# Attention and a squared-ReLU network in one program: integer weight splitting without the GpSimd sum, early queries turned by TensorE, copies whose engine the list picks

## The chip, the cores and the metric

The kernel runs on one core of a Trainium2 chip. Its engines work beside each other: TensorE (PE for matrix products, PEld for its weight loads), VectorE (DVE), ScalarE (ACT), GpSimd (POOL), and SyncE (SP), from whose queue all transfers start. The metric is the device time of one execution in microseconds (us).

## The reference

For 8 batches of 8 heads, 576 tokens and head dimension 64, the kernel computes a feature-map attention and passes the result, as 4608 tokens of width 512, through two matrix products with a squared ReLU between them.

```python
def phi(x):
    proj = np.einsum('bhsd,df->bhsf', x, w_phi)               # w_phi: 64 x 128
    proj = proj - np.max(np.abs(proj), axis=-1, keepdims=True)
    return np.concatenate([np.exp(proj), np.exp(-proj)], axis=-1)
q_p, k_p = (phi(q), phi(k))
kv = np.einsum('bhsf,bhsd->bhfd', k_p, v)
z = np.sum(k_p, axis=2)
num = np.einsum('bhsf,bhfd->bhsd', q_p, kv)
den = np.einsum('bhsf,bhf->bhs', q_p, z)[..., None] + 1e-06
attn = num / den                                              # then tokens x 512
h = x @ w_in                                                  # w_in: 512 x 2048
out = np.maximum(h, 0.0) ** 2 @ w_out                         # w_out: 2048 x 512
```

The weights w_in and w_out reach the kernel as 64-bit floating point, seen as pairs of 32-bit words.

## The kernel before

**Tiling.** Heads go in 32 pairs of two. A batch is four pairs. The network works on 18 chunks of 256 tokens, and on 8 slices of 256 features in each: 144 units, each a first product (gemm1, line 960, 24 products of half precision) and a second (gemm2, line 991, 12 products). A unit of chunk 0 needs slice f of both weights ready, and the attention of batch 0.

**Weights.** `prep` (line 400) makes one slice of w_in or w_out, 16 in all, from a raw tile of 1 MB: ACT takes the size of the upper word (`size`, line 421) and the low word as a number (`low`, 432), DVE shifts (`shift`, 424) and adds the sign (`join`, 428), POOL adds the rounded low part (`round_`, 435). After that, a slice of w_in has its largest value taken (453), goes through `power` (a PE product and four small DVE steps) and is split in two halves (ACT 457, DVE 459); a slice of w_out is split in two or three parts (ACT 477, POOL at the helper line 288, DVE 484).

**Attention.** The first six pairs go through `early` (line 605), the others through `visit` and `late`, which stand between the units of the network. In `early` the keys are projected (538, 544), shifted by their largest absolute value and put through the exponential (`keys`), multiplied with the values (594, 599) and with ones (626), and the sums turned (`flip`, 638). The queries are projected with tokens on the partitions (`q_main` 653, `q_tail` 659), so that DVE can take the largest value of each token (664, 668). Then `q_proj` projects them once more, with features on the partitions (682), and subtracts the largest values by products with a negative identity (`nident`, 691), in two halves of 288 tokens; ACT puts each half through two exponentials (698, 700) and the numerators (708) and denominators (726) follow. `tokens` (758) divides and writes the half-precision ring that gemm1 reads; for the first five pairs its product runs on POOL.

**What sets the order.** Every step is an `Op` of a `Plan` with an engine, a duration in us, its predecessors, its buffers and a rank. `Plan.order` is a list scheduler: each engine takes, of the steps that are ready, the one with the lowest rank; PE adds `STAY` to steps of another tiling mode, and a lock stretches DVE and POOL steps that meet. `improve` repeats it with shifted ranks and keeps the shortest plan. The order of the instructions on every engine is fixed by this plan before the program runs. Attention pairs are ranked 4.5 us apart, weight slices from 16.0 in steps of 1.0, units of the network from 36.0 in steps of 1.0.

Of the kernel before, what the change touches and what calls it, by code (L numbers as in the profile page):

```python
# [39 lines left out]
SH = S // 2  # L40
# [8 lines left out]
STAY = 6.0  # L49
TRIALS, SEED, MOVED = 400, 1, 70.0  # L50
WITH_DVE = 16
# [12 lines left out]
class Op:  # L64
    __slots__ = ("n", "eng", "us", "fn", "after", "uses", "rank", "land", "mode", "lock", "start", "end", "left", "next")

    def __init__(self, n, eng, us, fn, after, uses, rank, land, mode, lock):
        self.n, self.eng, self.us, self.fn, self.rank, self.land = n, eng, us, fn, rank, land
        self.mode, self.lock = mode, lock
        self.after, self.uses = [a for a in after if a is not None], list(uses)  # L70
        self.start = self.end = None


class Plan:

# [14 lines left out]
    def add(self, eng, us, fn, after=(), uses=(), rank=0.0, land=0.0, mode=WHOLE, lock=None):  # L90
        op = Op(len(self.ops), eng, us, fn, after, uses, rank, land, mode if isinstance(mode, tuple) else (mode, mode), lock)
        self.ops.append(op)
        return op
# [39 lines left out]
    def improve(self, trials, seed):  # L133
# [4 lines left out]
        for n in range(trials):  # L138
# [6 lines left out]
            if best is None or length <= best:  # L145
                best, plan = length, order
            else:
                for op, rank in old:
                    op.rank = rank
        return plan  # L150

    def order(self):
# [19 lines left out]
        def release(op, least=0.0):  # L172
            at = least
            for a in op.after:
                hop = self.HOP[a.eng] if a.eng != op.eng or a.land else 0.0
                at = max(at, a.end + a.land + hop)
            for tag, n in alone(op):
                at = max(at, open_at.get(tag, 0.0))
            heapq.heappush(waiting[op.eng], (at, op.rank, op.n))
# [5 lines left out]
        while done < len(self.ops):  # L185
            best = None
            for e in self.HOP:
                if not waiting[e] and not ready[e]:
                    continue
                t = free[e] if ready[e] else max(free[e], waiting[e][0][0])  # L190
                if best is None or t < best[0]:
                    best = t, e
            t, e = best
            while waiting[e] and waiting[e][0][0] <= t:
                _, rank, n = heapq.heappop(waiting[e])
                heapq.heappush(ready[e], (rank, n))
# [10 lines left out]
            op.start, op.end = t, t + op.us * (COLD if e == "PE" and t < 125.0 else 1.0)  # L207
            if op.lock is not None:
                if e == "POOL":
                    op.end = max(op.end, locked["DVE"] + op.us)  # L210
                else:
                    op.end += min(op.lock, max(0.0, locked["POOL"] - t))
# [44 lines left out]

def dve_us(n):
# [16 lines left out]
def tile_kernel(ctx, tc, qp, kp, vp, w_phi, w_in, w_out, out):  # L275
# [13 lines left out]

    def tiles(pool, tag, shape, dtype, bufs, first=0):  # L290
# [4 lines left out]
    nident = cp.tile([128, 128], F32, name="nident")  # L295
# [21 lines left out]
    pt_ = tiles(at, "pt", [128, 2, S], F32, 1, EARLY)  # L317
# [38 lines left out]
    for h in range(2):  # L356
# [5 lines left out]
    minus = P.add("DVE", 0.25, lambda: V.tensor_scalar(out=nident, in0=ident, scalar1=-1.0, scalar2=None, op0=ALU.mult),  # L362
                  [pool_start], [], 0.8)
# [5 lines left out]
    def power(src, dst, top, after, uses, rank):  # L369
# [15 lines left out]
        a = P.add("PE", 0.22, gather, after, key + [("pn", ("pw", n))], rank)  # L385
# [14 lines left out]
    def prep(n, f, of_in, rank):  # L400
# [22 lines left out]
        def shift():  # L423
            V.tensor_scalar(out=u(), in0=u(), scalar1=3, scalar2=0x7FFFFFF8,
                            op0=ALU.logical_shift_left, op1=ALU.bitwise_and)

        def join():
            V.scalar_tensor_tensor(out=u(), in0=high_w(), scalar=word(0x80000000), in1=u(),
                                   op0=ALU.bitwise_and, op1=ALU.bitwise_or)

        def low():
            A.activation(out=low_w(), in_=low_w().bitcast(U32), func=AF.Copy, scale=2.0 ** -29)

        def round_():
            G.tensor_tensor(out=u(), in0=u(), in1=low_w(), op=ALU.add)
# [10 lines left out]
        pool_prep.append(o)  # L446
        if of_in:
# [7 lines left out]
            o = home_read[home] = P.add("ACT", 1.25, most, [o], key, rank)  # L455
# [6 lines left out]
        else:  # L462
# [20 lines left out]
            if f < NFP - 2:  # L483
                last.append(P.add("DVE", 0.75, lambda: V.tensor_copy(out=wout[f][2], in_=value(2)), [o], key, rank, lock=0.45))  # L484
# [12 lines left out]
    def batch_scale(b, rank):  # L497
        last = []
        for i in range(NP):
            p = b * NP + i  # L500
            last.append(P.add("ACT", act_us(640) + 0.1, lambda p=p, i=i: A.activation(
# [20 lines left out]
        scale_of[b] = P.add("DVE", 0.5, tokens, [o], [], rank)  # L522
# [82 lines left out]
    def early(p):  # L605


        base, free = PER_PAIR * p, p < BANKS
# [24 lines left out]
        o = P.add("ACT", act_us(384), lambda: A.activation(out=kvs_[p], in_=pv_["s", p][:, 0:384], func=AF.Copy),  # L633
                  [o], [("pv", ("s", p)), ("kvs", p)], R(2.6))

        def flip():
# [4 lines left out]
        kz = P.add("ACT", act_us(384), lambda: A.activation(  # L641
            out=kz_[p], in_=pv_["t", p][:, 0:384], func=AF.Copy), [o], [("pv", ("t", p)), ("kz", p)], R(3.1))
# [3 lines left out]
        most = []  # L646
        q_to = lambda h: flat(ph_[2 * p + h]) if free else pp_["qt", p][:, h, :]
        q_use = [("ph", 2 * p + h) if free else ("pp", ("qt", p)) for h in range(2)]

# [11 lines left out]

        o = P.add("PE", 1.0, q_main, [q_load[p]], [("q", p)] + q_use, R(1.0), mode=ROWS)
        for h in range(2):
            most.append(P.add("DVE", dve_us(512), lambda h=h: V.tensor_reduce(
                out=qm_[p][:, 4 * h:4 * h + 4], in_=q_to(h).rearrange("p (t f) -> p t f", t=4),
                op=ALU.max, axis=AX.X, apply_absolute_value=True), [o], [q_use[h], ("qm", p)], R(1.1)))
        o = P.add("PE", 0.27, q_tail, [q_load[p]], [("q", p), ("pn", ("qt", p))], R(1.0), mode=COLS)
        most.append(P.add("DVE", dve_us(128), lambda: V.tensor_reduce(
            out=qm_[p][:, 8:9], in_=pn_["qt", p][:, 0:128], op=ALU.max, axis=AX.X,
            apply_absolute_value=True), [o], [("pn", ("qt", p)), ("qm", p)], R(1.1)))  # L670
# [4 lines left out]
        for c in range(2):  # L675
            n = 2 * p + c
            cs = slice(SH * c, SH * c + SH)
            pq = ("pp", ("q", n))

            def q_proj(n=n, cs=cs):  # L680
# [3 lines left out]
                for h in range(2):  # L684
                    for t in range(5):
                        lo, hi = max(cs.start, 128 * t), min(cs.stop, 128 * t + 128)
                        if lo < hi:

                            i, r, d = (4 * h + t, 0, lo - 128 * t) if t < 4 else (8, 64 * h, 64 * h)
                            rows = slice(r, 128 if t < 4 else r + 64)  # L690
                            PE.matmul(out=pp_["q", n][:, h, lo - cs.start:hi - cs.start],  # L691
# [391 lines left out]
```

## Time and profile before

| | |
|---|---|
| time, median of 3 runs | 1085.27 us (1084.39 to 1086.54) |
| the profiled execution: its own time | 1087.95 us |
| its span, from the first to the last instruction | 1085.8 us |
| PE busy | 1053.6 us (97%) |
| DVE busy | 744.8 us (69%) |
| ACT busy | 634.8 us (58%) |
| POOL busy | 183.4 us (17%) |
| mean granted clock of TensorE | 0.987 of full speed |

An engine's busy time is the time in which one of its instructions ran. The profile names the wait before an instruction and the engine whose work ended it. The granted clock is the share of full speed (2.4 GHz) that TensorE was given in a stretch; 0.5 is 1.2 GHz.

### The profile page before, as it was taken

What the parts mean: (1) busy time and instruction counts of PE and PEld (TensorE: products, weight loads), DVE (VectorE), ACT (ScalarE), POOL (GpSimd) and SP (SyncE); (2) the same over time, 40 slices, a digit from 0 to 9 for tenths busy, and PEclk for the clock granted to TensorE, in tenths of its full rate; (3) what the DMA queues carried; (4) which work ended last, traced back from release to release, by engine and by line L of the source; (5) the groups of instructions that cost most, each with busy time, mean ns of one, the idle gap of its engine ahead of it and who ended that gap; (6) DMA issues with size and microseconds to landing.
All of it is one profiled execution on the core that took longest, in us unless ns stands there. A gap on an engine that the chain in (4) does not pass through costs nothing.

```text
span 1085.8 us, 19895 instructions
## 1 busy us (share of the span) xinstructions
PE 1053.6 (97%) x7788; PEld 723.2 (67%) x7882; DVE 744.8 (69%) x1543; ACT 634.8 (58%) x1125; POOL 183.4 (17%) x87
## 2 busy tenths in 40 slices
PE   7997999999999999999999999999999999999997
PEld 5664666666666666666666666666666666777774
DVE  6588998888887887868777787867786865111111
ACT  6897864556566665666566666665555655333232
POOL 2344442111011111101111111111101111000000
PEclk9897999999999999999999999999999999999999
DMA  9643330222212222222112122222110101000000
GB/s 326 238 137 104 124 122 32 55 75 56 75 55 75 56 56 75 56 64 67 59 41 58 50 74 56 75 56 75 44 55 27 51 17 30 11 21 20 1 20 20
DMA packets 68289, 73.50 MB, mean 68 GB/s; under 512 B 36836, under 2 KB 41828, under 8 KB 68196
## 3 DMA queue, kind: packets, MB, share of 16 engines
q1 hardware_dynamic: 68196, 72.23, 21.8%
q8 instruction: 62, 1.02, 0.4%
q14 instruction: 31, 0.25, 0.1%
HBM read 59.18 MB, written 12.99 MB: 66 GB/s over the span
## 4 chain that ended last, share of the span: by engine, by line
PE 89%; DVE 4%; DMA 2%; ACT 2%; issue 2%; SPq 0%; POOL 0%; DVEq 0%; ACTq 0%; POOLq 0%
PE po L991 35%; PE ph L960 34%; PE pv L594 5%; PE pn L812 3%; PE pp L881 3%; PE pp L538 3%; PE pv L812 2%; PE pp L691 1%; PE pv L599 1%; DMA v<-in_vp_dram 1%; PE pn L544 1%; DMA raw0i<-in_w_in_dram 1%; DVE win L459 1%; DVE wl L484 1%; PE pn L708 1%
## 5 line engine op out<-in xcount | busy, mean ns | idle before, releaser
L960 PE MATMUL ph<-ring,win 128*128 128x256 f16 x3456 | 400.6, 273 | 2.6 <-DVE win L459 2.6
L960 PEld LDWEIGHTS <-win 128*128 128x128 f16 x3456 | 337.3, 98 | 69.8 <-issue 3.3
L969 ACT ACTIVATE r<-ph,cw 128x512 f32<-128x512 f32 x144 | 98.9, 687 | 239.0 <-PE ph L960 238.7
L894 POOL PARTITION_ALL_REDUCE mx<-pt x52 | 114.2, 2197 | 626.6 <-ACT pt L888 525.9
L288 DVE TENSOR_TENSOR gl<-ph,gh 128x512 bf16<-128x512 f32 x144 | 98.7, 686 | 157.8 <-ACT ph L978 154.8
L991 PE MATMUL po<-wh,gh 128*128 128x512 f32 x432 | 128.6, 419 | 0.0
L991 PE MATMUL po<-wl,gl 128*128 128x512 bf16 x420 | 110.2, 379 | 0.7
L991 PE MATMUL po<-wl,gh 128*128 128x512 bf16 x373 | 100.2, 381 | 3.8
L991 PEld LDWEIGHTS <-gl 128*128 128x128 bf16 x576 | 56.0, 97 | 69.6
L991 PEld LDWEIGHTS <-gh 128*128 128x128 bf16 x576 | 44.8, 98 | 74.1 <-issue 39.5
L971 ACT ACTIVATE gh<-r 128x512 fp32r<-128x512 f32 x144 | 90.8, 630 | 4.6
L991 PEld LDWEIGHTS po<-wh,gh 128*128 128x128 f32 x432 | 74.0, 189 | 18.6 <-issue 4.9
L991 PE MATMUL po<-wout,gh 128*128 128x512 f32 (+1 forms) x273 | 74.8, 405 | 1.2
L978 ACT ACTIVATE ph<-r 128x512 f32<-128x512 f32 x128 | 74.6, 583 | 0.0
L594 PE MATMUL pv<-e,v 128*64 128x256 f32 x512 | 64.3, 395 | 0.0
L834 ACT ACTIVATE n<-pn 128x320 f32<-128x320 f32 x26 | 11.4, 437 | 90.1 <-PE pn L812 90.1
L908 DVE SCALAR_TENSOR_TENSOR pt<-qe,zc,pt 128x576 f32<-128x576 f32 x52 | 42.3, 813 | 22.2 <-ACT pt L906 21.8
L560 ACT ACTIVATE e<-e 128x512 f32<-128x512 f32 x64 | 39.8, 621 | 24.8 <-DVE e L557 24.8
L288 DVE TENSOR_TENSOR qe<-pt,mx 128x576 f32<-128x576 f32 x52 | 39.2, 754 | 19.7 <-POOL mx L894 19.4
L594 PEld LDWEIGHTS pv<-e,v 128*64 128x64 f32 x512 | 37.0, 143 | 16.9 <-issue 3.8
L845 DVE STREAM_TRANSPOSE kvs<-pv 128x256 f32<-128x256 f32 x26 | 11.6, 445 | 45.8 <-PE pv L812 45.0
L906 ACT ACTIVATE pt<-qe,zc 128x576 f32<-128x576 f32 x52 | 40.0, 773 | 4.2
(204 smaller groups left out, 1483.4 us busy)
## 6 DMA issues: line engine op xcount, KB each, us to landing
v<-in_vp_dram SPq DMA_DIRECT2D x32, 320.0 KB
k<-in_kp_dram SPq DMA_DIRECT2D x32, 288.0 KB
q<-in_qp_dram SPq DMA_DIRECT2D x32, 288.0 KB
rb<-rd SPq DMA_DIRECT2D x64, 144.0 KB
out_dram<-o SPq DMA_DIRECT2D x36, 256.0 KB
td<-kvs SPq DMA_DIRECT2D x26, 128.0 KB
kz<-td SPq DMA_DIRECT2D x208, 16.0 KB
raw0i<-in_w_in_dram SPq DMA_DIRECT2D x1, 1024.0 KB
```

The lines of the kernel that those rows point to most:

```text
L288: eng.tensor_tensor(out=out_, in0=a, in1=b_, op=ALU.subtract)
L560: o = P.add("ACT", act_us(512), lambda n=n: A.activation(out=e_[n][:, :, 1, :], in_=e_[n][:, :, 0, :], func=AF.Exp, scale=-1.0), [o], [("e ...
L594: PE.matmul(out=to[64 * h:64 * h + 64, 0:256], lhsT=v_[p][:, t, h, :], rhs=e_[2 * p + h][:, t].rearrange("p s f -> p (s f)"), start=t == 0 ...
L812: PE.matmul(out=to[64 * h:64 * h + 64, :], lhsT=kz_[n][:, 128 * s_ + 64 * h:128 * s_ + 64 * h + 64], rhs=qe_[2 * n + h].rearrange("p (s x) ...
L894: o = P.add("POOL", par_us(S), lambda n=n, h=h: G.partition_all_reduce(mx_[n], pt_[p][:, h, :], channels=128, reduce_op=bass_isa.ReduceOp. ...
L906: o = P.add("ACT", act_us(S, 1), lambda h=h, qe=qe, y=y: A.activation(out=y(), in_=qe(0), func=AF.Copy, scale=zc_[p][:, 2 * h:2 * h + 1]), ...
L908: o = P.add("DVE", dve_us(S), lambda h=h, qe=qe, y=y: V.scalar_tensor_tensor(out=y(), in0=qe(1), scalar=zc_[p][:, 2 * h + 1:2 * h + 2], in ...
L960: PE.matmul(out=ph[:, j, :], lhsT=win[w][:, t, 128 * ff:128 * ff + 128], rhs=ring[half][x][:, t, c0:c0 + T], start=k == 0, stop=k == 3 * K ...
L969: o = P.add("ACT", act_us(512, 1), lambda: A.activation(out=r_[n], in_=ph_[bank], func=AF.Relu, scale=cw[:, f, 0:1]), [g1], [("ph", bank), ...
L971: sq = P.add("ACT", act_us(512), lambda: A.activation(out=gh_[n], in_=r_[n], func=AF.Square), [o], [("r", n), ("gh", n)], Q)
L978: o = P.add("ACT", act_us(512), lambda: A.activation(out=ph_[bank], in_=r_[n], func=AF.Square), [sq], [("ph", bank), ("r", n)], Q)
L991: PE.matmul(out=po_[po[i][1]], lhsT=g[:, j, 128 * i:128 * i + 128], rhs=w[:, j, :], start=(ff == 0 and s == 0), stop=(ff == 2 * NFP - 1 an ...
```

## The change

Three things change in what the program computes with, and one in how the plan is made.

**Weight words.** The steps `shift` and `round_` go. `low` makes a number from 0 to 7 of the low word in one ACT step (a scale and an offset, rounded to an integer), a new DVE step `ends` joins it with the sign of the upper word, in place of the raw low words, and `join` shifts the size by three bits and joins both, in one DVE step.

**Early queries.** `q_proj` goes, and `nident` with it. DVE subtracts the largest value from the projection that has tokens on the partitions (`less`, into `pt`), and TensorE turns the result by 12 transposes a pair (`q_turn`). ACT reads the turned halves of 288 from the same PSUM tile.

**Engines of copies.** `Plan.add` takes a second way for a step (`other`), on another engine. The list offers the step to both; the second engine sees it `LATER` = 2.0 us later, and whichever takes it first keeps it. It stands for the copies out of PSUM (ACT or DVE), the third part of w_out, the first half of the ring, the second squaring in the network (ACT first, DVE second; before, DVE for the first 16 units) and `tokens` of the first five pairs (DVE first, POOL second). Some durations in the plan are new too.

```diff
-        def shift():
-            V.tensor_scalar(out=u(), in0=u(), scalar1=3, scalar2=0x7FFFFFF8,
-                            op0=ALU.logical_shift_left, op1=ALU.bitwise_and)
+        def low():
+            A.activation(out=low_w(), in_=low_w().bitcast(U32), func=AF.Copy, scale=0.875 * 2.0 ** -29, bias=0.4995)
+
+        def ends():
+            V.scalar_tensor_tensor(out=low_w(), in0=high_w(), scalar=word(0x80000000), in1=low_w(),
+                                   op0=ALU.bitwise_and, op1=ALU.bitwise_or)
         def join():
-            V.scalar_tensor_tensor(out=u(), in0=high_w(), scalar=word(0x80000000), in1=u(),
-                                   op0=ALU.bitwise_and, op1=ALU.bitwise_or)
-        def low():
-            A.activation(out=low_w(), in_=low_w().bitcast(U32), func=AF.Copy, scale=2.0 ** -29)
-        def round_():
-            G.tensor_tensor(out=u(), in0=u(), in1=low_w(), op=ALU.add)
+            V.scalar_tensor_tensor(out=u(), in0=u(), scalar=3, in1=low_w(),
+                                   op0=ALU.logical_shift_left, op1=ALU.bitwise_or)
...
         l = P.add("ACT", 1.14, low, [ld], [], rank)
+        l = P.add("DVE", 1.22, ends, [l], [], rank, lock=4.0)
         o = P.add("ACT", 1.14, size, [ld], key, rank)
-        o = P.add("DVE", 0.70, shift, [o], key, rank, lock=0.45)
-        o = P.add("DVE", 1.22, join, [o], key, rank, lock=4.0)
-        o = P.add("POOL", 2.42, round_, [o, l], key, rank, lock=0.0)
+        o = P.add("DVE", 1.22, join, [o, l], key, rank, lock=4.0)
...
+        def most_of(src, i, n, o, use):
+            x = lambda: src().rearrange("p (t f) -> p t f", t=n)
+            o = P.add("DVE", dve_us(128 * n), lambda: V.tensor_reduce(
+                out=qm_[p][:, i:i + n], in_=x(), op=ALU.max, axis=AX.X, apply_absolute_value=True), [o], use + [("qm", p)], R(1.1))
+            less.append(P.add("DVE", dve_us(128 * n), lambda: V.tensor_tensor(
+                out=flat(pt_[p])[:, 128 * i:128 * (i + n)].rearrange("p (t f) -> p t f", t=n), in0=x(),
+                in1=qm_[p][:, i:i + n].unsqueeze(2).to_broadcast([128, n, 128]), op=ALU.subtract),
+                [o], use + [("qm", p), ("pt", p)], R(1.1)))
...
-                    PE.matmul(out=pp_["q", n][:, h, 0:SH], lhsT=wst[64 * h:64 * h + 64, :],
-                              rhs=q_[p][64 * h:64 * h + 64, cs], start=True, stop=False)
...
-                            PE.matmul(out=pp_["q", n][:, h, lo - cs.start:hi - cs.start],
-                                      lhsT=qm_[p][rows, i:i + 1].to_broadcast([rows.stop - r, 128]),
-                                      rhs=nident[rows, d:d + hi - lo], start=False, stop=hi == cs.stop)
+                    for t in range(3 - c):
+                        PE.transpose(pp_["q", n][:, h, 128 * t:128 * t + 128], ut(4 * h + 2 * c + t), ident)
+                if c:
+                    for h in range(2):
+                        rows = slice(64 * h, 64 * h + 64)
+                        PE.transpose(pp_["q", n][:, h, 256:320], ut(8)[rows, :], ident[rows, rows])
...
+    def copy(n, to, of):
+        return (("ACT", out_us(n), lambda: A.activation(out=to(), in_=of(), func=AF.Copy)),
+                ("DVE", dve_us(n), lambda: V.tensor_copy(out=to(), in_=of()), None))
```

The first place in the order is TensorE on the queries of pair 0 (`pp` is the PSUM tile of the half, `qm` the largest values, `pt` the new tile of differences). Before, the first half:

```order
L682 MATMUL pp_264<-q_118,wraw 128x288 x2
L691 MATMUL pp_264<-nident,qm_171 128x128 x2
L691 MATMUL pp_264<-nident,qm_171 128x32
L691 MATMUL pp_264<-nident,qm_171 128x128 x2
L691 MATMUL pp_264<-nident,qm_171 128x32
L638 MATMUL pv_284<-ident,kvs_275 128x128 x3
```

And now both halves, in the order of the program:

```order
L714 MATMUL pp_221<-ident,pt_187 128x128 x6
L624 MATMUL pv_199<-et_182,v_119 64x256 x2
...
L714 MATMUL pp_307<-ident,pt_187 128x128 x4
L718 MATMUL pp_307<-ident,pt_187 128x64 x2
L664 MATMUL pv_317<-ident,kvs_281 128x128 x3
```

Eight products of a half, of which the profile shows 16 records, became six transposes.

The second place is TensorE just ahead of the first unit of the network (`win` is w_in's first half, `ring` the tokens; 538 and 563 are pair 5's keys, 708 and 733 numerators, 726 and 750 denominators, 594 and 626 values and ones). Before:

```order
L708 MATMUL pn_1065<-qe_981,kz_983 64x288 x4
L594 MATMUL pv_1076<-e_1029,v_342 64x256
...
L653 MATMUL pp_1090<-wraw,q_882 128x128 x8
...
L599 MATMUL pv_1076<-et_930,v_342 64x256 x2
...
L626 MATMUL pv_1076<-et_930,mask 32x128 x4
L659 MATMUL pn_1150<-wraw,q_882 64x128 x2
L960 LDWEIGHTS win_77
```

Now:

```order
L714 MATMUL pp_995<-ident,pt_880 128x128 x4
L718 MATMUL pp_995<-ident,pt_880 128x64 x2
L733 MATMUL pn_1017<-qe_974,kz_976 64x288 x4
L563 MATMUL pp_1026<-wraw,k_690 128x128 x8
L733 MATMUL pv_1039<-qe_1010,kz_976 64x288 x4
L750 MATMUL pn_1050<-qe_974,kz_976 32x288
...
L986 LDWEIGHTS win_76
```

The values, the ones and the query projection of pair 5 stood before the first unit and now stand behind it.

The third place is DVE around a slice of the weights (`raw3i` is slice 3 of w_in, `raw1o` slice 1 of w_out, `u` the joined words). Before:

```order
L459 SCALAR_TENSOR_TENSOR win_78<-u_458,cw,win_77 128x4x256
L668 TENSOR_REDUCE qm_868<-pn_877 128x1
L424 TENSOR_SCALAR u_880<-u_880 128x1024
L428 SCALAR_TENSOR_TENSOR u_880<-raw2o,u_880 128x1024
L564 TENSOR_REDUCE kmt_928<-pn_901 128x1
```

Now:

```order
L456 SCALAR_TENSOR_TENSOR raw3i<-raw3i 128x1024
L691 TENSOR_REDUCE qm_631<-pn_760 128x1
L483 SCALAR_TENSOR_TENSOR win_77<-u_360,cw,win_76 128x4x256
L693 TENSOR_TENSOR pt_688<-pn_760,qm_631 128x128
L582 TENSOR_TENSOR e_797<-po_622,km_739 128x4x128
L456 SCALAR_TENSOR_TENSOR raw1o<-raw1o 128x1024
L460 SCALAR_TENSOR_TENSOR u_787<-u_787,raw1o 128x1024
L589 TENSOR_REDUCE kmt_835<-pn_822 128x1
L460 SCALAR_TENSOR_TENSOR u_808<-u_808,raw3i 128x1024
```

A slice has two joins on DVE (456, 460) in place of a shift and a join, the differences of the queries (693) stand among them, and POOL has no step between the joins and ACT.

## Rows read from the trace of the kernel before

**Rows 1.** Busy time by stage: stretch, length, PE, PEld, DVE, ACT, POOL, clock, DMA.

```profile
0.00:22.00 22.00, 15.28 (x157) 12.05 (x159) 12.24 (x24) 12.78 (x22) 2.99 (x7) 0.92 0.92 332
22.00:109.60 87.60, 78.62 (x785) 52.52 (x783) 66.67 (x105) 72.55 (x123) 36.43 (x18) 0.88 0.50 166
109.60:165.40 55.80, 51.62 (x383) 35.31 (x386) 51.88 (x79) 41.99 (x65) 27.36 (x11) 1.00 0.37 119
...
200.00:1000.00 800.00, 794.76 (x5717) 545.08 (x5794) 570.96 (x1251) 466.23 (x847) 109.83 (x50) 1.00 0.19 53
```

**Rows 2.** TensorE in order of time: start, length, engine, line, tiles, count.

```profile
18.93 0.76 PE L682 MATMUL pp<-q,wraw 64*128 64x288 f32 x4
19.62 1.52 PE L691 MATMUL pp<-nident,qm 128*128 128x128 f32 x12
20.98 0.53 PE L638 MATMUL pv<-ident,kvs 128*128 128x128 f32 x3
21.43 0.44 PE L544 MATMUL pn<-wraw,k 128*64 128x128 f32 x4
...
57.74 0.76 PE L682 MATMUL pp<-q,wraw 64*128 64x288 f32 x4
58.43 2.07 PE L691 MATMUL pp<-nident,qm 128*128 128x96 f32 x12
60.43 0.49 PE L375 MATMUL pn<-ident,wm 128*128 128x128 f32 x2
...
95.51 1.33 PE L682 MATMUL pp<-q,wraw 64*128 64x288 f32 x4 [2.53 <-DVE e L557]
96.77 3.60 PE L691 MATMUL pp<-nident,qm 128*128 128x96 f32 x12
100.30 2.19 PE L708 MATMUL pn<-qe,kz 128*64 128x288 f32 x8
102.27 3.01 PE L594 MATMUL pv<-e,v 128*64 128x256 f32 x16
...
106.30 1.18 PE L726 MATMUL pn<-qe,kz 128*32 128x288 f32 x16
107.41 0.65 PE L599 MATMUL pv<-et,v 128*64 128x256 f32 x4
...
109.59 2.79 PE L960 MATMUL ph<-ring,win 128*128 128x256 f16 x24
...
165.39 4.24 PE L960 MATMUL ph<-ring,win 128*128 128x256 f16 x22 [2.62 <-DVE win L459]
```

**Rows 3.** Single instructions of the line of the turned sums (638).

```profile
L638 PE MATMUL pv<-ident,kvs x18: 272/273/328, 21.0 to 113.7; 128*128 128x128 f32 x18
```

**Rows 4.** ScalarE from 22 to 109.6 us, grouped by line.

```profile
L698 ACT ACTIVATE qe<-pp 128x576 f32<-128x576 f32 x10 | 6.4, 643 | 4.0 <-PE pp L691 4.0
L457 ACT ACTIVATE win<-u,cw 128x1024 f16<-128x1024 f32 x5 | 5.7, 1150 | 0.9 <-DVE cw L383 0.8
...
L501 ACT ACTIVATE sx<-v 128x640 bf16<-128x640 f32 x6 | 4.4, 740 | 0.8 <-DMA v<-in_vp_dram 0.8
L477 ACT ACTIVATE wh<-u 128x1024 fp32r<-128x1024 f32 x4 | 4.2, 1052 | 1.2 <-POOL u L435 1.2
```

**Rows 5.** VectorE from 22 to 109.6 us, grouped by line.

```profile
L424 DVE TENSOR_SCALAR u<-u 128x1024 int32<-128x1024 int32 x9 | 10.9, 1206 | 2.6 <-ACT u L421 2.6
...
L557 DVE TENSOR_TENSOR e<-po,km 128x512 f32<-128x512 f32 x6 | 4.1, 682 | 5.5 <-PE pv L626 5.5
...
L428 DVE SCALAR_TENSOR_TENSOR u<-raw4i,u 128x1024 int32<-128x1024 int32 x1 | 3.4, 3410 | 0.0
...
L428 DVE SCALAR_TENSOR_TENSOR u<-raw3o,u 128x1024 int32<-128x1024 int32 x1 | 1.2, 1224 | 0.0
```

**Rows 6.** Granted clock in two stretches of the attention stage; columns as above.

```profile
24.00:34.00 10.00, 9.71 (x50) 6.01 (x54) 3.04 (x11) 6.11 (x14) 2.40 (x1) 0.66 1.00 381
...
87.00:105.30 18.30, 15.15 (x76) 9.22 (x76) 14.88 (x22) 14.97 (x22) 8.02 (x4) 0.63 0.37 106
```

More of the change, by code (lines that the diff above doesn't have):

```diff
@@ L145, in improve @@
             if best is None or length <= best:
-                best, plan = length, order
+                best, plan = length, [(op, op.eng) for op in order]
             else:
@@ L149, in improve @@
                     op.rank = rank
-        return plan
+        for op, eng in plan:
+            op.take(eng)
+        return [op for op, _ in plan]
     def order(self):
@@ L170, in alone, with release, gone @@
             return [key for key in op.uses if key[0] in self.single]
[L172 to L179, printed above, removed]
+        def release(op):
+            least = max([open_at.get(tag, 0.0) for tag, n in alone(op)], default=0.0)
+            for eng in op.ways:
+                at = least
+                for a in op.after:
+                    at = max(at, a.end + a.land + (self.HOP[a.eng] if a.eng != eng or a.land else 0.0))
+                second = eng != next(iter(op.ways))
+                heapq.heappush(waiting[eng], (at + LATER * second, op.rank + BEHIND * second, op.n))
+        def gone(n):
+            return self.ops[n].start is not None
         for op in self.ops:
@@ L483, in prep @@
             if f < NFP - 2:
-                last.append(P.add("DVE", 0.75, lambda: V.tensor_copy(out=wout[f][2], in_=value(2)), [o], key, rank, lock=0.45))
+                last.append(P.add("DVE", 0.75, lambda: V.tensor_copy(out=wout[f][2], in_=value(2)), [o], key, rank, lock=0.6,
+                                  other=("ACT", 1.06, lambda: A.activation(out=wout[f][2], in_=value(2), func=AF.Copy), None)))
             return last
@@ L632, in early @@
         o = P.add("PE", 1.66, ends, [o, exp_t[p]], kv, R(2.5), mode=(COLS, STRIPS))
-        o = P.add("ACT", act_us(384), lambda: A.activation(out=kvs_[p], in_=pv_["s", p][:, 0:384], func=AF.Copy),
-                  [o], [("pv", ("s", p)), ("kvs", p)], R(2.6))
+        first, second = copy(384, lambda: kvs_[p], lambda: pv_["s", p][:, 0:384])
+        o = P.add(*first, [o], [("pv", ("s", p)), ("kvs", p)], R(2.6), other=second)
         def flip():
@@ L713, in early @@
                       R(4.0 + 0.8 * c), mode=COLS)
-            nums.append(P.add("ACT", act_us(SH), lambda c=c: A.activation(
-                out=n_[p][:, SH * c:SH * c + SH], in_=banks[c][0]["n", p][:, 0:SH], func=AF.Copy),
-                [o], [banks[c][1], ("n", p)], R(4.1 + 0.8 * c)))
+            first, second = copy(SH, lambda c=c: n_[p][:, SH * c:SH * c + SH], lambda c=c: banks[c][0]["n", p][:, 0:SH])
+            nums.append(P.add(*first, [o], [banks[c][1], ("n", p)], R(4.1 + 0.8 * c), other=second))
         def dens():
@@ L731, in early @@
                   R(5.6), mode=STRIPS)
-        o = P.add("ACT", act_us(SH), lambda: A.activation(
-            out=sx_["d", p][:, 0:SH], in_=pn_["d", p][:, 0:SH], func=AF.Copy), [o], [("pn", ("d", p))] + use, R(5.7))
+        first, second = copy(SH, lambda: sx_["d", p][:, 0:SH], lambda: pn_["d", p][:, 0:SH])
+        o = P.add(*first, [o], [("pn", ("d", p))] + use, R(5.7), other=second)
         o = P.add("SP", 0.1, lambda: SP.dma_start(
@@ L833, in visit @@
             for bank, key, x, lo, hi in ((pn_, pn, 0, 0, N0), (pv_, pv, 256, N0, S)):
-                nums.append(P.add("ACT", act_us(hi - lo), lambda bank=bank, x=x, lo=lo, hi=hi: A.activation(
-                    out=n_[n][:, lo:hi], in_=bank["a", i][:, x:x + hi - lo], func=AF.Copy), [v], [key, ("n", n)], rank + 0.1))
+                first, second = copy(hi - lo, lambda lo=lo, hi=hi: n_[n][:, lo:hi],
+                                     lambda bank=bank, x=x, lo=lo, hi=hi: bank["a", i][:, x:x + hi - lo])
+                nums.append(P.add(*first, [v], [key, ("n", n)], rank + 0.1, other=second))
         if s is not None:
```

114 lines of the change are left out of this document (56 added, 58 removed).

## The prediction

> **What bounds the kernel now.** I read the page's engine shares first, then the stages, then TensorE in order of time, and last the two engines that feed it. TensorE is busy 1053.6 of 1085.8 us, so 32.2 us are all that waits can give back; the rest is its own work. By stage [rows 1] it idles 6.7 us before 22, 9.0 us from 22 to 109.6, 4.2 us up to 165.4, and only 5.2 us in the 800 us from 200 to 1000. Where these borders lie shows in the timeline [rows 2]: at 109.59 the first unit of the network starts, and at 165.39 TensorE stands for the last time for a weight slice (2.62 us for the second half of w_in). From there on the kernel is bound by TensorE, and the end comes earlier by as much as the unit at 165.39 does, with the work behind it unchanged.
>
> The stage from 22 to 109.6 is different: TensorE is busy 90% of it, ACT 83%, DVE 76% [rows 1]. No engine is full; the steps of a pair go from one to the next, beside the weight slices, which load ACT and DVE. So work taken from TensorE there is worth something only as far as ACT and DVE can follow. What the reader is to take from the rows: TensorE's total shrinks by a known amount, and the question is how much of it turns into idle time ahead of the first unit.
>
> **TensorE: early queries.** A first half of `q_proj` takes 2.05 us (18.93 to 20.98) and a second half 2.69 us (57.74 to 60.43) at full clock [rows 2]. Six pairs make 28.4 us; the one at 95.51 took 4.79 us, 2.1 more, at a lower clock. Removed: 30.5 us. The transposes that take its place are the instruction of line 638, of which three go in 0.45 us (20.98 to 21.43) [rows 2], 0.15 each: 72 of them, 10.8 us, 0.9 a half. TensorE saves 19.7 us. The other end is the length of a single one, 0.27 us [rows 3]: 19.7 us for 72, if each waits for the one before; only runs of three are in the trace. I take 0.15, since those three overlapped.
>
> The Trainium skill ("TensorE: Matmul & The Clock Gate", section on PE-mode transpose) speaks against this: it gives about 275 ns for a transpose inside a kernel, most of it the latency of reading the data. The single records here have just that length, but their starts are closer; by the page's figure as a price of each, an estimate, the saving would be 10.7 us and not 19.7.
>
> Of the twelve halves one runs before 22, nine from 22 to 109.6 (four first, five second: 8.2 + 13.5 + 2.1 = 23.8 us, replaced by 8.1) and two behind it (4.7 us, replaced by 1.8). The saving in front of 22 is lost: there the loads set the pace. So 15.7 us less work stand in the attention stage and 2.9 in the next.
>
> **The attention stage.** The new order also puts pair 5's values, ones and query projection behind the first unit, and one numerator ahead. These took 4.0 us (102.27 to 106.30) and 2.2 us (107.41 to 109.59) [rows 2], partly slow; less a numerator I take 5 us moved, no gain and no loss in total. TensorE's work ahead of the first unit falls from 78.6 to about 58 us, and it is no longer what sets the stage.
>
> ACT: ahead of the first unit the new order has two slices fewer begun (two `low`, two `size`), one `win` fewer and one third part of w_out more: four passes at about 1.15 us, 4.6 us; three passes over v fewer (0.74 each, 2.2) and two exponentials fewer (0.64 each, 1.3) [rows 4]. 72.6 becomes 64.5 us. Of its 15 idle us, 4.0 were for line 691 and 1.2 for POOL's sum [rows 4], both gone; without these it was busy 88%. 64.5 at 88% is 73 us.
>
> DVE: ten differences of 512 at 0.68 us as the key's [rows 5], and five of a quarter of it, 8.2 us. A shift cost 1.21 us on the mean, a join 1.22 [rows 5]; two joins instead come out even, while two slices fewer give back 4.9. Four products of `tokens` come from POOL, 0.77 each by the same row's rate, 3.1. One `win` and one w_out copy fewer, about 2. The join that took 3.41 instead of 1.22 us while POOL was at work [rows 5] gives 2.2. Sum: 66.7 + 8.2 - 4.9 + 3.1 - 2 - 2.2 = 68.9 us. It is bounded below by some 63 (the shifts' and splits' stalls beside POOL go as well) and above by 81: no row shows a DVE step that writes every second word, as `ends` does; at twice the price its ten steps cost 12 us more. I take the 1.22 of the join, which already reads every second word. DVE has been 93% busy in the stage behind (51.9 of 55.8) [rows 1]; at that share 68.9 us need 74.
>
> ACT at 73 and DVE at 74 side by side won't both be that full: I take 76 us. The first unit starts at 98 and not 109.6, 11.6 us earlier. GpSimd's sum leaves each slice's path, which is why I let ACT and DVE keep their shares though TensorE's cover shrinks.
>
> **Up to 165.4.** This stage gets the 5 us moved, loses 2.9, and the squarings of the units go from DVE, which was full there, to ACT, at 42.0 of 55.8 [rows 1]. With seven sums fewer on POOL, I let 2 of its 4.2 idle us go; the rest, and the wait for the last slice, stay. 5 - 2.9 - 2 is zero: the last wait moves by the same 11.6 us.
>
> **Behind it.** 128 squarings of 144 stood on ACT already, the rest and two large copies that DVE now has lie under a TensorE that is 99% busy; cost and gain nothing. If that cover failed, 5.2 us of idle in 800 would show it. `nident` and the plan's new durations cost nothing by themselves.
>
> **Sum.** 30.5 us of products out, 10.8 in, 1.1 lost in front, 9 more idle in the attention stage, 2 less behind it: 11.6 us. The span goes to 1074.2; with the 2.15 us around it, 1076.4 in the profiled execution, which was 2.7 us above the median of the timed runs (1087.95 against 1085.27). In the terms of the median: 1073.7 us.
>
> **Rivals.**
> *More of it arrives.* ACT and DVE at 95% (68 and 66 us at the lower bound): the first unit at 91 to 92, 18 us earlier, 1066 to 1068 us. For it: DVE was at 93% once [rows 1], and the waits of ACT for TensorE and POOL go. Against: attention pairs still pass through three engines in turn. With TensorE's whole 19.7 us and 2 of idle it ends at 1064.
>
> *DVE takes it all.* If `ends` costs twice, DVE has 81 us, at 93% a stage of 87, and TensorE waits out what it saved: 1083 to 1086 us. For it: DVE gets 8.2 us of differences on the path of each query, between projection and turning. Against: one row's join with spaced words at the normal rate. The change would do what it says and buy nothing.
>
> *Transposes at full length.* They cost 8.9 us more. In the attention stage TensorE would have 65 of 76 us, which hides most of it; in the worst case all is on the path, 1075 to 1083 us.
>
> *Slower, by the clock.* From 24 to 34 the granted clock was 0.66 and from 87 to 105.3 it was 0.63 [rows 6], which means half of full speed (1.2 GHz) for most of these, and a wait of TensorE of 2.53 us (95.51) lies in the second [rows 2]. More idle time ahead of the first unit can spread this. At full clock the stage's work before was 78.6 less 0.34 x 9.7 and 0.37 x 15.2, 69.7 us; after, 69.7 - 21.7 + 8.1 - 4.5, about 52 us. With a tenth of waits it fills 87.6 us again at a mean clock of 0.66, the point from which the change loses; at 0.6 the stage has 96 us and the kernel takes 1093 us, at half speed throughout about 1110. For it: two stretches of 28 us do it already. Against: in such a stretch TensorE is itself the bound (9.7 busy of 10), which ends its waits.
>
> **How the numbers follow.** The forecast, 1069 to 1080 us, has 0.60; more of it, 0.15; transposes at full length, 0.05; DVE takes it all, 0.13; the clock, 0.07. A difference below 0.2%, 2.2 us, can't be told from no change here. Faster by more than that: 0.60 + 0.15 + 0.05 and a third of DVE's case, 0.84; within it, the rest of that case, 0.09; slower 0.07. The range that leaves out the clock, most of DVE's case and the extreme of the second is 1064 to 1083 us.
>
> **What would show it.** Right: line 714 and 718 at 0.15 us a transpose; the first unit near 98; the last wait for a weight slice near 154; from there the same rows as before, and TensorE's busy time near 1034 us. DVE's rival: the new line 456 at 2.4 us and DVE over 95% ahead of the first unit. The clock's: a granted clock below 0.7 over most of 22 to 98. It is wrong if TensorE idles more than 20 us between 22 and the first unit, or if waits appear behind the last slice.

## The result, and the profile after

The changed kernel takes 1076.24 us (median of 4 runs, 1075.53 to 1077.26) against 1085.90 (1084.39 to 1088.01), a ratio of 0.9902 (95% interval 0.9876 to 0.9927). The profiled execution has a span of 1074.5 us, 11.3 less than before. The number came out as forecast. The cause did not, and most of what follows is about that.

The page's engine shares, after:

```profile
PE 1038.8 (97%) x7762; PEld 707.2 (66%) x7762; DVE 738.3 (69%) x1558; ACT 635.6 (59%) x1132; POOL 136.4 (13%) x66
```

The stages, with the columns of [rows 1]; the borders are the first unit of the network and the unit that stands where the last wait for a weight slice was:

```profile
0.00:22.00 22.00, 15.65 (x167) 12.25 (x167) 14.01 (x28) 13.75 (x24) 0.68 (x6) 1.00 0.90 312
...
22.00:98.40 76.40, 57.55 (x601) 36.17 (x600) 58.15 (x104) 63.98 (x112) 7.50 (x3) 0.87 0.54 182
98.40:156.30 57.90, 54.84 (x450) 36.96 (x447) 52.68 (x93) 49.71 (x77) 11.56 (x4) 0.97 0.39 128
200.00:1000.00 800.00, 800.00 (x5793) 545.30 (x5791) 564.10 (x1233) 456.62 (x831) 105.36 (x48) 1.00 0.18 52
```

Against [rows 1], TensorE's work ahead of the first unit fell from 78.6 to 57.6 us. It now idles 18.9 us there, not 9.0. ScalarE is busy 84% of the stage, VectorE 76%: no engine is full. From 200 to 1000 there is no idle time at all.

TensorE in order of time, with the columns of [rows 2]:

```profile
42.76 0.88 PE L714 MATMUL pp<-ident,pt 128*128 128x128 f32 x6
43.47 0.39 PE L402 MATMUL pn<-ident,wm 128*128 128x128 f32 x2
48.49 0.90 PE L664 MATMUL pv<-ident,kvs 128*128 128x128 f32 x3 [4.63 <-ACT kvs L317]
...
98.35 2.79 PE L986 MATMUL ph<-ring,win 128*128 128x256 f16 x24
...
156.26 2.79 PE L986 MATMUL ph<-ring,win 128*128 128x256 f16 x24
```

A half of the queries, 2.05 to 2.69 us at full clock in [rows 2], takes 0.71 us here from its start to that of the next step. The first unit starts at 98.35. The unit at 156.26 finds its slice ready, where the one at 165.39 in [rows 2] waited 2.62 us.

VectorE ahead of the first unit, grouped by line:

```profile
L693 DVE TENSOR_TENSOR pt<-ph,qm 128x512 f32<-128x512 f32 x8 | 5.3, 682 | 0.0
L483 DVE SCALAR_TENSOR_TENSOR win<-u,cw,win 128x1024 f16<-128x1024 f32 x4 | 5.1, 1277 | 0.0
L785 DVE TENSOR_TENSOR rb<-n,rb 128x576 f32<-128x576 f32 x4 | 4.9, 1213 | 2.8 <-DMA rb<-rd 2.8
...
L807 DVE SCALAR_TENSOR_TENSOR ring<-rb,cb,ring 128x576 f16<-128x576 f32 x4 | 3.2, 805 | 0.6 <-ACT ring L804 0.6
...
L456 DVE SCALAR_TENSOR_TENSOR raw3i<-raw3i 128x1024 int32<-128x1024 int32 x1 | 1.2, 1218 | 0.0
...
L460 DVE SCALAR_TENSOR_TENSOR u<-u,raw3i 128x1024 int32<-128x1024 int32 x1 | 1.2, 1215 | 0.0
```

The new `ends` (456) costs what a join costs, and no join stalls as the one of [rows 5] did. Two steps that the change does not touch are cheaper per piece. In the kernel before, in its own stage from 22 to 109.6:

```profile
L459 DVE SCALAR_TENSOR_TENSOR win<-u,cw,win 128x1024 f16<-128x1024 f32 x5 | 9.8, 1963 | 0.0
...
L784 DVE SCALAR_TENSOR_TENSOR ring<-rb,cb,ring 128x576 f16<-128x576 f32 x4 | 4.8, 1195 | 0.0
```

The split of w_in went from 1.96 to 1.28 us, the second half of the ring from 1.20 to 0.81, while GpSimd's busy time in the stage went from 36.4 to 7.5 us. The Trainium skill ("SBUF — State Buffer", section on the two separate sides) says that a VectorE step with two inputs in SBUF and a GpSimd step that reads SBUF lock each other out for a whole instruction; these rows agree.

What TensorE waited for in the kernel after (engine, tile, line, releaser: total, times, longest, in us):

```profile
PE po L563 <- DMA k<-in_kp_dram: 6.3, 2, 4.3
PE pv L664 <- ACT kvs L317: 4.6, 1, 4.6
PE pn L733 <- DVE et L592: 4.5, 1, 4.5
PE pn L402 <- DVE pw L406: 3.0, 1, 3.0
```

The first row is the loads at the start. The next two are attention steps (the turned sums and the numerators), and the last is the product in `power` for a weight slice, at 119.94 us, behind the first unit. Each waits once, for ScalarE or VectorE, which reached its step late.

### The profile page after: what moved, and what is told of

The parts are those of the page before. It is cut to its first block, busy times and chain, and to the rows that moved or that the text cites. A ratio compares the mean times of both kernels' runs of the same rounds, so it can differ in the third digit from the quotient of the medians.

```text
span 1074.5 us, 19722 instructions
## 1 busy us (share of the span) xinstructions
PE 1038.8 (97%) x7762; PEld 707.2 (66%) x7762; DVE 738.3 (69%) x1558; ACT 635.6 (59%) x1132; POOL 136.4 (13%) x66
## 4 chain that ended last, share of the span: by engine, by line
PE 90%; DVE 5%; DMA 3%; issue 1%; ACT 0%; SPq 0%; DVEq 0%; ACTq 0%
PE po L1013 37%; PE ph L986 35%; PE pv L619 5%; PE pp L563 3%; PE pn L837 3%; PE pp L907 3%; PE pv L837 2%; PE pv L624 1%; PE pn L569 1%; DVE wl L508 1%; DMA den<-sx 1%; DMA k<-in_kp_dram 1%; DMA v<-in_vp_dram 1%; DMA rd<-rc 1%; DVE u L460 1%
## 5 line engine op out<-in xcount | busy, mean ns | idle before, releaser
L1013 PE MATMUL po<-wl,gh 128*128 128x512 bf16 x432 | 112.8, 384 | 0.0
L999 ACT ACTIVATE ph<-r 128x512 f32<-128x512 f32 x144 | 84.0, 583 | 0.1
L317 ACT ACTIVATE n<-pn 128x320 f32<-128x320 f32 (+1 forms) x32 | 13.8, 431 | 100.7 <-PE pn L837 98.4
L934 DVE SCALAR_TENSOR_TENSOR pt<-qe,zc,pt 128x576 f32<-128x576 f32 x52 | 42.2, 812 | 18.9 <-ACT pt L932 18.2
L925 ACT ACTIVATE qe<-qe 128x576 f32<-128x576 f32 x52 | 34.9, 671 | 13.9 <-DVE qe L313 13.9
L871 DVE STREAM_TRANSPOSE kvs<-pv 128x256 f32<-128x256 f32 x26 | 11.6, 445 | 44.3 <-PE pv L837 42.4
```

What stands on the lines that cost most here:

```text
L925: o = P.add("ACT", act_us(S), lambda qe=qe: A.activation(out=qe(1), in_=qe(0), func=AF.Exp, scale=-1.0), [o], [("qe", n)], R(RQ + 0.4))
L934: o = P.add("DVE", dve_us(S), lambda h=h, qe=qe, y=y: V.scalar_tensor_tensor(out=y(), in0=qe(1), scalar=zc_[p][:, 2 * h + 1:2 * h + 2], in ...
L999: o = P.add("ACT", 0.59, lambda: A.activation(out=ph_[bank], in_=r_[n], func=AF.Square), [o], [("ph", bank), ("r", n)], Q, other=("DVE", 0 ...
L1013: PE.matmul(out=po_[po[i][1]], lhsT=g[:, j, 128 * i:128 * i + 128], rhs=w[:, j, :], start=(ff == 0 and s == 0), stop=(ff == 2 * NFP - 1 an ...
```

## The experiments

Two theories stood at the start. *Load*: how much VectorE and ScalarE have to do sets when TensorE can run. *Order*: the engines have room, and the time depends on which instruction queues behind which late one. Each ratio below is to the kernel before on the same chip. Where the text says "the same order", the plan's durations were left alone, so that the instructions keep the order of the changed kernel. In all others the plan was made anew.

**Queries alone.** The kernel before with `q_turn` and the differences, nothing else. It ran with the plan's second seed:

```diff
-TRIALS, SEED, MOVED = 400, 1, 70.0
+TRIALS, SEED, MOVED = 400, 2, 70.0
-            def q_proj(n=n, cs=cs):
+            def q_turn(n=n, c=c):
```

> Only the early queries are turned (weights and copies as before; the search over plans starts from seed 2, not 1). Load theory (ACT and DVE together set the stage ahead of the first unit): TensorE loses 20 us of work, DVE gains 8 us beside POOL's sums that still stall it, so the first unit starts near 104 and the kernel gains 4 to 6 us (1080 to 1082). Order theory (what stands in a queue behind a late transfer sets the stage, the engines have room): the 20 us come through by half, 8 to 11 us (1075 to 1078).

1092.72 us, ratio 1.0046 (1.0030 to 1.0063). Neither theory had expected a slower kernel.

**Weight words alone.** The kernel before with `low`, `ends` and the new `join`:

```diff
-        o = P.add("DVE", 0.70, shift, [o], key, rank, lock=0.45)
-        o = P.add("POOL", 2.42, round_, [o, l], key, rank, lock=0.0)
+        l = P.add("DVE", 1.22, ends, [l], [], rank, lock=4.0)
```

> Only the weight words are joined the new way (queries and copies as before). Load theory: DVE loses its stalls beside POOL (7 us or more), but TensorE keeps all its work and is 90% busy in the stage, so 2 to 5 us are gained (1081 to 1084). Order theory: between 0 and 2 us (1084 to 1086).

1083.75 us, ratio 0.9974 (0.9955 to 0.9993), 2.8 us better, in load's range.

**Engines of copies alone.** The changed kernel with the old queries and the old weight words:

```diff
-            def q_turn(n=n, c=c):
+            def q_proj(n=n, cs=cs):
-        l = P.add("DVE", 1.22, ends, [l], [], rank, lock=4.0)
+        o = P.add("POOL", 2.42, round_, [o, l], key, rank, lock=0.0)
```

> Only the choice of engines by the list and the plan's new durations (weights and queries as before). Both theories: no work is removed; load theory 0 to 3 us gained (1083 to 1086), order theory anything from 3 us gained to 3 us lost.

1082.49 us, ratio 0.9951 (0.9934 to 0.9967), 5.3 us better, more than either theory had expected.

**Another seed, changed kernel.** The same work in another order, with the engines of the copies chosen anew:

```diff
-TRIALS, SEED, MOVED = 400, 1, 70.0
+TRIALS, SEED, MOVED = 400, 2, 70.0
```

> The changed kernel with the search over plans started from seed 2 in place of 1: the same work in another order. Load theory: within 2 us of 1076. Order theory: 3 us or more away from it, to either side, with other waits ahead of the first unit.

1070.28 us, ratio 0.9847 (0.9824 to 0.9870): 6.0 us better by the ratios, and the best of all versions. Order had expected a move of that size, load had not.

**Another seed, kernel before.** The same edit there:

> The kernel before, with another seed for the search of its plan and nothing else: the same instructions in another order. If load sets the time: 1082 to 1089 us, the same within 0.3%, since no engine's work changes. If the order of the plan decides: 5 us or more to either side, as the changed kernel moved by 6 us with its second seed. It also says how the kernel with the queries alone, which ran with this seed, is to be read.

1092.02 us, ratio 1.0048 (1.0026 to 1.0071), 5.2 us worse. So a plan is worth 5 to 6 us to either side. Load did not expect this, and no difference of less can be read from two kernels with different plans. It also says how the queries alone are to be read: with the same seed they stand at 1.0046 against 1.0048, which is no difference, though their plan is another one too.

**`ends` twice**, the same order:

```diff
+        def ends_twice():
+            ends()
+            ends()
-        l = P.add("DVE", 1.22, ends, [l], [], rank, lock=4.0)
+        l = P.add("DVE", 1.22, ends_twice, [l], [], rank, lock=4.0)
```

> The changed kernel in its own order, with the new step `ends` issued twice on DVE for each of the 16 weight slices (the second writes what stands there already): 1.2 us more on DVE a slice, some 10 slices ahead of the first unit. Load theory (DVE full): about 9 to 11 us later than the changed kernel, 1085 to 1087. Order theory (DVE has a quarter of the stage to spare, waits for others set it): 2 to 5 us later, 1078 to 1081, since part of the extra steps falls into DVE's waits.

1091.53 us, ratio 1.0056 (1.0036 to 1.0077): 15 to 17 us more for 16 steps of 1.22 us, 19.5 us. About 0.8 us for each on VectorE, above what load expected. The second step also lies on each slice's path, so this is the price of load and path together; `size` twice, below, is read the same way.

**The transposes twice**, the same order:

```diff
-P.add("PE", 0.8, q_turn,
+P.add("PE", 0.8, lambda q_turn=q_turn: (q_turn(), q_turn()),
```

> The changed kernel in its own order, with the transposes of the early queries issued twice: about 10 us more on TensorE, 8 of them ahead of the first unit. If TensorE set that stage: 9 to 10 us later, 1085 to 1086. Load theory (ACT and DVE set it): only the two halves behind the first unit count, 1 to 3 us later, 1077 to 1079. Order theory: 3 to 5 us, since every turning lies on the path of a pair's chain between DVE and ACT.

1076.50 us, ratio 0.9915 (0.9892 to 0.9938), 1.4 us more, with the interval overlapping that of the kernel after. In its timeline six transposes follow six at 0.79 us:

```profile
22.35 0.66 PE L714 MATMUL pp<-ident,pt 128*128 128x128 f32 x4
22.94 0.28 PE L718 MATMUL pp<-ident,pt 64*128 64x64 f32 x2
23.14 0.66 PE L714 MATMUL pp<-ident,pt 128*128 128x128 f32 x4
```

So 72 more transposes are some 9.5 us of TensorE, and cost 1.4, as load expected: TensorE has room ahead of the first unit. Part of that room is the clock's. From 22 to 180 us (columns of [rows 1]) this run's trace has

```profile
22.00:180.00 158.00, 141.93 (x1314) 95.80 (x1313) 134.98 (x243) 130.77 (x218) 24.91 (x10) 0.97 0.44 147
```

and the kernel after 136.09 us of work at 0.92: of 8 to 9 us of transposes added there, 5.8 show as more busy time, at a higher granted clock.

**`size` twice**, the same order:

```diff
-P.add("ACT", 1.14, size, [ld]
+P.add("ACT", 1.14, lambda: (size(), size()), [ld]
```

> The changed kernel in its own order, with ACT's `size` issued twice for each of the 16 weight slices: 1.1 us more on ACT a slice, some 10 ahead of the first unit, where ACT is busy 64 of 76 us. Load theory (ACT the fuller of the two): 8 to 11 us later, 1084 to 1087. Order theory: 3 to 6 us, 1079 to 1082.

1083.98 us, ratio 0.9983 (0.9969 to 0.9997): 8.8 us more for 16 passes of 1.15 us, 18.4 us, as load expected; about 0.5 for each on ScalarE.

**Own scratch for the pass over v.** In the kernel after, ScalarE's longest wait ahead of the first unit was for a transfer that still read the scratch tile `sx`:

```profile
ACT sx L526 <- DMA den<-sx: 4.5, 1, 4.5
```

A tile of its own takes that wait away, the same order:

```diff
+    vx_ = tiles(at, "vx", [128, 640], BF16, 1, None)
-out=sx_["va", p].bitcast(BF16)[:, 0:640], in_=v_[p]
+out=vx_["va", p], in_=v_[p]
```

> The changed kernel in its own order, with a tile of its own for what ACT writes while it takes the largest value of v, so that this step no longer waits until the denominators' transfer has read the tile it shared (4.5 us of ACT's wait at 47 us, and a wait of TensorE of 4.6 us behind it, in the changed kernel's trace). Order theory: 3 to 5 us earlier, 1071 to 1073. Load theory: ACT only catches up what it has to do anyway, 0 to 1.5 us earlier.

1073.54 us, ratio 0.9897 (0.9871 to 0.9923). The wait is gone from ScalarE, the first unit starts at 95.84 and not 98.35, and the gain of 0.5 us by the ratios is inside the intervals. Two ratios with such intervals leave the difference uncertain by near 4 us, so both theories' ranges stay possible and this run decides nothing.

**All but the weight words.** The changed kernel with `shift`, `join` and `round_` of before:

```diff
-        l = P.add("DVE", 1.22, ends, [l], [], rank, lock=4.0)
+        o = P.add("POOL", 2.42, round_, [o, l], key, rank, lock=0.0)
```

> The changed kernel with the old weight words (shift, join and GpSimd's sum), the new queries and the free choice of engines kept; the plan is made anew. If the load of VectorE and ScalarE sets the stage ahead of the first unit: GpSimd's sums come back beside VectorE, the splits of w_in go from 1.27 to about 2.3 us and the joins stall again, some 9 us more on VectorE over both stages, at 0.8 us each 7 us: 1083 us, first unit near 103. If the parts simply add up, the weight words are worth what they were alone, 0.26%: 1079 us. If the order of the plan decides: anywhere from 1070 to 1082, with VectorE's busy time saying nothing of it.

1080.74 us, ratio 0.9952 (0.9935 to 0.9970), between what load (1083) and the plain sum of the parts (1079) gave, and inside the range of order.

**All but the queries.** The changed kernel with `q_proj` and `nident` of before:

```diff
-            def q_turn(n=n, c=c):
+            def q_proj(n=n, cs=cs):
```

> The changed kernel with the old projection of the early queries (products with a negative identity), the new weight words and the free choice of engines kept; the plan is made anew. If load sets the stage: TensorE gets 15.7 us back ahead of the first unit (57.6 to 73) and VectorE loses 8 us of differences (58 to 50); TensorE is again the fullest at about 73 of 82 us, and the kernel takes 1080 to 1084 us, first unit near 103. If the parts add up: queries alone were slower by 0.46%, so without them 1071 us. If the order of the plan decides: 1070 to 1082.

1074.15 us, ratio 0.9881 (0.9846 to 0.9916): the whole gain without the queries. Load had expected 1080 to 1084 here, because it made TensorE the fullest engine again. It was, and that did no harm. The same stretch, 22 to 180 us, of the kernel before, the kernel after, and this one (columns of [rows 1]):

```profile
22.00:180.00 158.00, 144.77 (x1251) 97.48 (x1256) 129.26 (x205) 120.01 (x199) 68.40 (x30) 0.92 0.42 136
```

```profile
22.00:180.00 158.00, 136.09 (x1219) 89.87 (x1219) 130.29 (x236) 130.27 (x217) 25.96 (x10) 0.92 0.43 142
```

```profile
22.00:50.00 28.00, 27.81 (x346) 19.43 (x342) 17.17 (x35) 25.95 (x47) 2.36 (x1) 1.00 0.84 298
22.00:180.00 158.00, 151.02 (x1405) 103.76 (x1410) 131.71 (x236) 132.96 (x223) 23.88 (x10) 0.98 0.44 143
```

With the old queries TensorE idles 7.0 us in this stretch at a mean clock of 0.98; with the new ones 21.9 us at 0.92. Fifteen us of the saving became idle time, and the lower clock, 0.06 of some 140 us, cost about 8 more, an estimate: together the 20 us saved, and a little over. The two other comparisons of the queries show the same. The kernel before with its second seed, then the queries alone; the copies alone, then all but the weight words:

```profile
22.00:180.00 158.00, 135.11 (x1218) 91.27 (x1223) 130.49 (x209) 119.85 (x197) 67.45 (x29) 0.96 0.43 143
```

```profile
22.00:180.00 158.00, 124.81 (x1108) 81.39 (x1112) 128.91 (x215) 116.23 (x193) 66.05 (x27) 0.90 0.43 138
```

```profile
22.00:180.00 158.00, 144.61 (x1296) 100.11 (x1303) 129.47 (x224) 132.19 (x221) 64.19 (x25) 0.96 0.43 140
```

```profile
22.00:180.00 158.00, 132.30 (x1199) 88.87 (x1205) 129.26 (x220) 129.47 (x215) 64.35 (x25) 0.91 0.44 142
```

Idle time rose by 10 and by 12 us, and the clock fell from 0.96 to 0.90 and 0.91. Behind 180 TensorE is full in both kernels of the first comparison; of the other four only the queries alone wait there for more than 1 us (2.8). From 22 to 50 TensorE with the old queries (all but the queries, above) runs nearly without a gap at full clock, where the kernel after has 21.2 of 28 us at 0.91:

```profile
22.00:50.00 28.00, 21.22 (x248) 13.94 (x248) 18.43 (x37) 21.57 (x43) 0.00 (x0) 0.91 0.87 311
```

**w_out's third part on ScalarE**, with the second seed. Five casts of it on VectorE took 1.93 us each beside GpSimd:

```diff
-                last.append(P.add("DVE", 0.75, lambda: V.tensor_copy(out=wout[f][2], in_=value(2)), [o], key, rank, lock=0.6,
-                                  other=("ACT", 1.06, lambda: A.activation(out=wout[f][2], in_=value(2), func=AF.Copy), None)))
+                last.append(P.add("ACT", 1.06, lambda: A.activation(out=wout[f][2], in_=value(2), func=AF.Copy), [o], key, rank))
```

> The changed kernel with the plan's second seed (1070.3 us) and the third part of w_out's slices always on ScalarE. In the changed kernel five of these casts took 1.93 us each on VectorE beside GpSimd's subtractions, 9.6 us ahead of the last weight slice. If load sets the time: 9.6 us less on VectorE at 0.8 against 5.3 us more on ScalarE at 0.5: some 5 us, 1065 us. If the order of the plan decides: 1070 us with 6 to either side.

1077.66 us, ratio 0.9916 (0.9886 to 0.9946): 7 us slower than the second seed without the edit, where load expected 5 faster. TensorE's waits in it:

```profile
PE pn L732 <- DVE pw L406: 6.0, 2, 5.8
PE pp L679 <- issue: 4.4, 1, 4.4
PE pn L568 <- issue: 3.2, 1, 3.2
```

One wait of 5.8 us for a small VectorE step is as much as the edit was to bring. The sensitivities measured at a fixed order do not forecast a kernel whose plan is made anew.

**What they say together.** Three comparisons change the queries alone:

| | without | with | with less without |
|---|---|---|---|
| old weights, old copies (both second seed) | 1.0048 | 1.0046 | -0.0002 |
| old weights, new copies | 0.9951 | 0.9952 | +0.0001 |
| new weights, new copies | 0.9881 | 0.9902 | +0.0021 |

A minus is a gain from the queries. Taking the intervals as independent, these are uncertain by 0.003, 0.002 and 0.004, and by the luck of a plan. Had the queries been worth the 11 us, plans would have had to hide them three times; a gain of a few us can't be excluded. The weight words made a difference of -0.0026 alone, -0.0070 on the new copies and -0.0050 on copies and queries (0.9974; 0.9881 against 0.9951; 0.9902 against 0.9952). The copies made -0.0049 alone and -0.0093 on the new weight words (0.9951; 0.9881 against 0.9974). Each is a gain in every comparison; the sizes, 3 to 8 us and 5 to 10 us, spread by no more than a plan's luck, and the smallest are within it. All plans together say it more firmly: with neither weight words nor copies the kernels stand at 1.0000, 1.0046 and 1.0048, with one of the two at 0.9951, 0.9952 and 0.9974, with both at 0.9847 to 0.9916, and the three groups do not overlap, whatever the queries and the seed. By what path the weight words bring theirs is less clear. The split of w_in, a step that GpSimd's sums hold up, took 2.35, 2.20, 1.89, 1.72 and 1.58 us on the mean of eight where the sums are kept (before, its second seed, copies alone, all but the weight words, queries alone), and 1.76, 1.43, 1.41 and 1.27 where they are gone (weight words alone, all but the queries, the second seed, after). It is shorter without the sums, but the ranges meet, and the queries alone, at 1.58, are among the slowest kernels.

What the copies do is in the rows of 22 to 180: ScalarE does 120.0 us of work there before, 119.9 with the second seed, 116.2 with the queries alone and 123.4 with the weight words alone. With the choice of engines it does 132.2 (copies alone), 129.5 (all but the weight words), 133.0 (all but the queries) and 130.3 (after), at 128 to 132 of VectorE throughout. The two engines get through some 10 us more by then, as they would if the list fills ScalarE's gaps. That fits load, but it is not shown to be the cause: no run took this one thing away from the copies, which also have new durations in the plan.

## Why the number was right and its cause was not

*TensorE's saving.* The products that went were 31.3 us and not 30.5, because the half at 24.29 us lay at the lower clock too and took 3.44 us up to the next step; transposes came at 0.12 to 0.13 us against the 0.15 taken. The single records still last 0.27 us, and that is refuted as a price. The Trainium skill ("TensorE: Matmul & The Clock Gate", section on PE-mode transpose) gives about 275 ns: by these rows that is the length of one, not the distance between two. TensorE's total is 1038.8 us, not 1034, because the total of before was too low (last section): with some 5.8 us more for it, the saving is about the forecast 20.

*The first unit and the last wait.* The first unit starts at 98.35 against 98. ScalarE's load is 63.98 us against 64.5, in part by luck: of the passes over the weights and over v it lost some 3.8 us, not 6.8, and the exponentials of the keys, which the forecast did not count, fell by 3.1. The unit that waited last moved by 9.1 us and not 11.6, with its wait gone. Some 2 us more came behind that point, where the forecast had nothing: the 22 products at 165.39 took 4.24 us [rows 2] and the 24 at 156.26 now take 2.79, and the granted clock from the one to 200 us was 0.95, from the other 1.00.

*VectorE's load.* This is the term that was mis-sized: 58.15 us ahead of the first unit, against 68.9 and a lower bound of 63. The edited weight steps came as worked out: shifts and joins of 24.0 us became 17.0, 7.0 less, as the forecast had with 4.9 and 2.2. The differences took 6.4 in place of 8.2: eight of 512 and four small ones, not ten and five, since some ran before 22. (At the forecast's own prices, 0.68 and a quarter of it, ten and five make 7.7; the small ones took 0.28.) `tokens` cost 4.9 and not 3.1. Not seen were: the split of w_in (4.7 us less for one fewer), ring and denominator steps (1.6 and 1.9 less, four of each in both), cheaper beside a GpSimd that is mostly idle; two casts fewer (1.5 less); and steps of the pairs that now stand outside the stretch (some 3). The lower bound named such stalls without counting them. It did not hurt the sum, by luck, because a second error met it: VectorE was busy 76% of the stage and not the 93% on which the 74 us rested.

*The ledger.* It forecast 9 us more idle time ahead of the first unit and 2 less behind. Measured, it is 9.9 more ahead and 1.1 less up to 156.3; from 22 to 180 idle went from 13.2 to 21.9 us, 8.7 more, at the same clock. As a balance between these two kernels the sum is right.

*The step that failed* is the reading of that balance: "30.5 us of products out, 10.8 in" as where the gain comes from. It took TensorE's own work as what held this stage, in which TensorE was 90% busy. With the old products still in, TensorE did 151.0 us of work in the 158 us, 96%, and the end came no later. So the saving bought nothing that three comparisons could find. The gain came from what the forecast let pass in half a sentence ("GpSimd's sum leaves each slice's path") and from what its sum gave no gain at all, the choice of engines. Two errors cancelled: a saving that did not arrive, and parts that were worth about as much.

*The rivals.* "DVE takes it all" falls with line 456 at 1.22 us; that VectorE is the dear engine, 0.8 of each us added, was its true part. The clock's rival falls with 0.87 from 22 to 98; its true part is that in all three comparisons the queries lowered the clock. "More of it arrives" is what the second seed came near, by its plan alone: first unit at 93.21, 1070.3 us.

*Left open.* Whether the 0.44% by which weights and copies together exceed the sum of their single effects is interplay or plan; by which steps the weight words and the copies bring their gain; and why one plan beats another by 6 us. None of these was isolated.

## What to carry to other kernels

A balance of busy and idle time between two kernels says where the time stands, not which edit put it there: take the edit out of the changed kernel as well as putting it alone into the old one. Where a planner remakes the order, run another seed of both kernels before reading a difference smaller than theirs. An engine that is 90% busy amid waits may still have room: add work to each engine at a fixed order and see which of them charges for it, with the granted clock beside the time.

## What the runs showed that was not expected

- Transposes follow each other at 0.12 to 0.13 us while each record lasts 0.27.
- TensorE's idle time in a full stretch can be missing records. From 180 to 1060 the kernel after has 880.00 us busy with 6346 products; before it is 874.24 with 6265, while the weight loads of TensorE (6343 and 6349) and the work of VectorE and ScalarE are alike. The 5.2 us of idle time in [rows 1] behind 200 were of this kind, and no wait in the profile stands for them.
- The clock gave back part of what the old queries cost: from 22 to 180 it was 0.96, 0.96 and 0.98 with them and 0.90, 0.91 and 0.92 without, and 0.97 with the transposes doubled. No rule comes of it: the kernel before had 0.92 there with 144.8 us of work, the weight words alone 0.96 with 144.6.
